# A new order of all steps for attention and a feed-forward layer on one core, with the loads of a pair's values cut into three steps

## The chip, the cores and the metric

The kernel runs on one core of one Trainium2 chip. The metric is the device time of one execution in microseconds (us). Three executions of the kernel before took 1015.79, 1017.2 and 1020.79 us; the median is 1017.2 us.

The core has five engines that each take their instructions in program order and meet only at semaphores: PE (matrix products; its weight loads are listed apart as PEld), DVE (elementwise work and reductions), ACT (exponential, Gelu, copies), POOL (more elementwise work, and a few DMA issues) and SP, which here only issues DMAs.

## The reference

The reference is sliding-window attention with 32 global tokens (8 batches, 8 heads, 512 local tokens, head size 64, window 32), followed by a feed-forward layer of 4352 tokens:

```
s_g  = scale * q_g @ concat(k_g, k_l)^T          # global rows see everything
out_g = softmax(s_g) @ concat(v_g, v_l)
s_l  = concat(scale * q_l @ k_g^T, where(|i-j| <= 32, scale * q_l @ k_l^T, -1e9))
out_l = softmax(s_l) @ concat(v_g, v_l)
x = concat(out_g, out_l) with the heads side by side      # 4352 x 512
h = x @ w_in                                     # 512 -> 2048
out = (0.5 * h * (1 + erf(h / sqrt(2)))) @ w_out # 2048 -> 512
```

All data are float32 and all of it is computed.

## The kernel before

**Tiling.** The attention is cut into 64 units (batch, half of the 512 tokens, pair of heads). A unit loads keys, queries and values, transposes keys and queries, makes scores on PE (`s`, L893), masks them with a running maximum on DVE (L912), takes exponentials on ACT (`a_t`, L766), normalises on DVE, transposes the weights on PE (`t`, L967 to L970), copies and splits them on ACT and DVE (`at`, L597 and L987) and multiplies by the values (`o`, L1004). Products are done in three parts, high*high, high*low and low*high, so every operand is copied (high part) and subtracted (low part) first. The global rows have steps of their own (`gu_*`).

**The feed-forward layer** is cut into 17 blocks of 256 tokens: 16 (batch, half) blocks and one for all global tokens. The first five take the plain way (`h`, L1193 or L1197 to L1199). The other twelve go in six groups of two blocks, in which a seven-product scheme is used: 28 products per group (`ml_p`, `hb`, L1301), each of 12 matmuls, and each with a tile `rt` of prepared weights, 512 KB, read from DRAM by one DMA of SP (`r_l`, L1262) into one of four buffers. So there are 168 `rt` loads, and one can go out only when the product four earlier has ended. The second product of the layer (`acc`, L1339 in the first block, L1347 to L1349 after) goes on between them.

**The loads.** SP issues nearly all DMAs, in one queue: keys and queries of a unit (four DMAs each, L713 and L718, rows of 32 floats), values of two units (`load_v`, `vr`, nine DMAs, L738 to L749: two of 128 rows, three and four of short rows), values for the global rows (`gu_load`, six DMAs, L1118 and L1120), the weights (`wraw`, L622 and L626, 512 KB each) and `rt`.

**What sets the order.** `plan` lists all steps: engine, what a step needs, what buffers it takes and frees, a duration from `DUR`. The order itself is a table of numbers, `SEQ`, that was searched offline; the program below only reads it. Each number names a step and the engine that does it, and the steps are written out in that order, so each engine's queue is the table's order of its steps. `DUR`, `LAT`, `iss`, due times and sizes serve the search and the table of names; they change nothing in the program when the table is fixed. The eight units of the first batch go a way of their own: keys and queries are transposed on PE (`kp`, `qp`, L806 to L814) and copied out of PSUM (`kt`, `qt`, L597) in two buffers that turn round.

## Time and profile before

| what | us |
|---|---|
| median of the three runs | 1017.2 |
| lowest, highest | 1015.79, 1020.79 |
| the profiled execution's own time | 1019.66 |
| its span | 1017.0 |
| PE busy | 992.0 |
| DVE busy | 716.4 |
| ACT busy | 727.4 |
| POOL busy | 406.2 |

The span runs from the first to the last instruction; 2.66 us of the execution lie around it. The ends of matmuls are modelled, so a PE that is shown busy is not always at its pace; a wait that the profile does show on PE is lost time. TensorE's granted clock was 0.999 of full speed over the span, which is its level of 2.4 GHz.

### The profile page before, as it was taken

The numbers are of one execution on the slowest core, as the hardware profiler recorded it, in microseconds if no ns is written. First come the engines' busy times: TensorE is split into PE (matmuls) and PEld (weight loads), VectorE is DVE, ScalarE is ACT, GpSimd is POOL, SyncE is SP. The second block draws the span as 40 slices with busy tenths as digits, with TensorE's granted clock in tenths as the row PEclk, the third lists the DMA queues.
The fourth block names the chain that finished last, engine by engine and source line by source line (L and its number), as shares of the span: only waits on it lengthen the run. The fifth ranks groups of instructions, "written<-read, shape, count | busy, mean of one in ns | idle before, by whom it ended". The sixth has DMA issues, their size and how long they took to land.

```text
span 1017.0 us, 21214 instructions
## 1 busy us (share of the span) xinstructions
PE 992.0 (98%) x6712; PEld 864.1 (85%) x6712; DVE 716.4 (70%) x2220; ACT 727.4 (72%) x1709; POOL 406.2 (40%) x431
## 2 busy tenths in 40 slices
PE   6999999999999999989999999999999999999998
PEld 3877688999889987988899988898898988998986
DVE  4899887688878888768888886687978786211111
ACT  4899889777987778776788877786888776343321
POOL 6231345433355324434543455234452454225223
PEclk9999999999999999999999999999999999999999
DMA  9996133455355798875678656986378746672641
GB/s 199 293 276 165 28 70 57 106 113 123 89 143 129 205 288 244 232 212 135 164 210 234 177 136 175 255 207 176 86 215 246 205 107 190 228 258 87 217 170 36
DMA packets 307728, 175.05 MB, mean 172 GB/s; under 512 B 256256, under 2 KB 279040, under 8 KB 307616
## 3 DMA queue, kind: packets, MB, share of 16 engines
q1 hardware_dynamic: 304064, 171.07, 61.7%
q0 software_dynamic: 1344, 1.97, 0.8%
q8 instruction: 53, 0.87, 0.4%
q10 hardware_dynamic: 2208, 0.66, 0.3%
q14 instruction: 59, 0.48, 0.2%
HBM read 149.49 MB, written 24.12 MB: 171 GB/s over the span
## 4 chain that ended last, share of the span: by engine, by line
PE 76%; DMA 12%; DVE 4%; ACT 4%; SPq 3%; issue 1%; POOL 0%; DVEq 0%; ACTq 0%; POOLq 0%
PE hb L1301 17%; PE acc L1347 10%; PE acc L1348 9%; PE acc L1349 9%; PE s L893 4%; PE o L1004 4%; DMA rt<-wd 3%; PE h L1197 3%; PE h L1198 3%; PE h L1199 3%; PE t L967 2%; PE acc L1339 2%; DMA raws<-in_q_l_dram 2%; PE h L1193 2%; PE sg L1050 2%; PE go L1137 1%
## 5 line engine op out<-in xcount | busy, mean ns | idle before, releaser
L1347 PE MATMUL acc<-wh,gh 128*128 128x512 f32 x512 | 207.2, 405 | 0.1
L1349 PE MATMUL acc<-wl,gh 128*128 128x512 f32 x512 | 202.4, 395 | 0.0
L1348 PE MATMUL acc<-wh,gl 128*128 128x512 f32 x512 | 201.8, 394 | 0.2 <-POOL gl L604 0.2
L604 POOL TENSOR_TENSOR gl<-gf,gh 128x512 fp32r<-128x512 f32 x80 | 103.9, 1298 | 222.8 <-DVE gh L599 73.5
L1301 PE MATMUL hb<-fh,rt 128*128 128x256 f32 x960 | 184.8, 281 | 4.2 <-DMA rt<-wd 3.7
L1301 PEld LDWEIGHTS hb<-fh,rt 128*128 128x128 f32 x960 | 152.8, 188 | 8.5 <-ACT sgr L766 1.8
L1301 PE MATMUL hb<-fl,rt 128*128 128x256 f32 x480 | 133.4, 278 | 0.0
L766 ACT ACTIVATE a_t<-a_t,sm 128x192 f32<-128x192 f32 (+1 forms) x256 | 116.8, 458 | 2.7 <-DVE sm L918 2.0
L1349 PEld LDWEIGHTS acc<-wl,gh 128*128 128x128 f32 x512 | 96.1, 188 | 21.7
L1347 PEld LDWEIGHTS acc<-wh,gh 128*128 128x128 f32 x512 | 96.4, 188 | 16.0 <-ACT ob L597 0.9
L1348 PEld LDWEIGHTS acc<-wh,gl 128*128 128x128 f32 x512 | 96.5, 188 | 14.4 <-POOL gl L604 0.8
L604 POOL TENSOR_TENSOR vs<-vr,vs 128x512 fp32r<-128x512 f32 x56 | 72.3, 1290 | 81.2 <-ACT vs L597 16.6
L912 DVE CUSTOM_DVE_ANT_0 a_t<-s,mask 128x192 f32<-128x192 f32 (+1 forms) x256 | 81.1, 368 | 19.1 <-PE s L893 18.5
L1301 PEld LDWEIGHTS hb<-fl,rt 128*128 128x128 f32 x480 | 90.3, 188 | 1.4
L766 ACT ACT_TABLE_LOAD x69 | 88.5, 1283 | 1.2
L987 DVE TENSOR_TENSOR at<-t,at 128x512 fp32r<-128x512 f32 (+1 forms) x112 | 68.3, 618 | 21.3 <-ACT at L597 20.2
L604 POOL TENSOR_TENSOR gl<-gq,gh 128x512 fp32r<-128x512 f32 x47 | 61.2, 1302 | 50.4 <-ACT gh L597 19.1
L597 ACT ACTIVATE at<-t 128x512 fp32r<-128x512 f32 (+1 forms) x112 | 59.8, 541 | 25.4 <-PE t L968 12.0
L1301 PE MATMUL hb<-xf,rt 128*128 128x256 f32 x576 | 75.0, 281 | 1.7 <-ACT s L597 1.6
L1301 PEld LDWEIGHTS hb<-xf,rt 128*128 128x128 f32 x576 | 70.8, 188 | 5.1 <-ACT s L597 2.0
L1197 PE MATMUL h<-xh,wh 128*128 128x256 f32 x256 | 74.9, 292 | 0.0
L1004 PE MATMUL o<-at,vs 128*128 128x256 f32 x448 | 71.8, 284 | 0.9 <-DVE gsm L1083 0.6
(191 smaller groups left out, 2287.7 us busy)
## 6 DMA issues: line engine op xcount, KB each, us to landing
rt<-wd SPq DMA_DIRECT2D x168, 512.0 KB, 4.5
wraw<-in_moe_w_in_dram SPq DMA_DIRECT2D x16, 512.0 KB, 6.9
wraw<-in_moe_w_out_dram SPq DMA_DIRECT2D x16, 512.0 KB, 6.0
raws<-in_v_l_dram SPq DMA_DIRECT2D x64, 128.0 KB, 3.2
out_dram<-ob SPq DMA_DIRECT2D x32, 256.0 KB, 2.5
raws<-in_k_l_dram SPq DMA_DIRECT2D x224, 36.0 KB, 2.6
raws<-in_q_l_dram SPq DMA_DIRECT2D x224, 32.0 KB, 2.5
vr<-in_v_l_dram SPq DMA_DIRECT2D x48, 128.0 KB, 3.7
```

The lines of the kernel that those rows point to most:

```text
L597: nc.scalar.activation(out=out, in_=in_, func=AF.Copy)
L604: (nc.vector if e == "v" else nc.gpsimd).tensor_sub(**kw)
L766: nc.scalar.activation(func=func, **kw)
L893: nc.tensor.matmul(out=st[u, "s", jj][:, c:c + w], lhsT=qq[pr, qt * P:qt * P + P], rhs=kk[pr, k0:k0 + w], start=(i == 0 and n == 0), stop= ...
L912: nc.vector.tensor_tensor_reduce(out=a_t[:, j, aoff[half][i]:aoff[half][i] + w], in0=s[:, c:c + w], in1=masks[half][i], scale=1.0, scalar= ...
L987: nc.vector.tensor_sub(out=at[:, 1], in0=st.pop((u, "t", j))[:, :n * P].rearrange("p (n q) -> p n q", q=P), in1=at.bitcast(F32)[:, 0])
L1004: nc.tensor.matmul(out=o[:, :, qsl], lhsT=l.rearrange("p s e -> p (s e)"), rhs=r, start=(n == 0), stop=(n == 3), skip_group_check=True)
L1197: nc.tensor.matmul(out=h, lhsT=hi, rhs=xh, start=(c == 0 and f % 2 == 0), stop=False, skip_group_check=True)
L1301: nc.tensor.matmul(out=h[:, r], lhsT=a, rhs=b, start=(i in (1, 5) and r == 0 and c == 0 and n == 0), stop=(c == 1 and n == 2), skip_group_ ...
L1347: nc.tensor.matmul(out=acc[t], lhsT=gh[:, f % 2, tsl], rhs=hi, start=(f == 0), stop=False)
L1348: nc.tensor.matmul(out=acc[t], lhsT=gl[:, f % 2, tsl], rhs=hi, start=False, stop=False)
L1349: nc.tensor.matmul(out=acc[t], lhsT=gh[:, f % 2, tsl], rhs=lo, start=False, stop=(f == NF - 1))
```

## The change

`DUR` and the two latencies of the search get other values (most durations of ACT and DVE 0.07 to 0.08 us lower, the latency behind a PE step 0.16 instead of 0.4), issues of late loads are counted a little longer, and the whole of `SEQ` is another table. The values of a pair of units, nine DMAs in one step, become three steps of two, three and four DMAs, which the table can put apart; the values of the global rows, six DMAs, become two steps of two and four. No instruction of PE is added or removed; a few steps change their engine.

```diff
 DUR = {
-    "k2": 0.49,
+    "k2": 0.42,
 ...
-LAT = {"t": 0.4}
-LAT0 = 0.15
+LAT = {"t": 0.16}
+LAT0 = 0.13
 ...
 SEQ = (
 ...
-    "eLcG}`+sUo5k3"
 ...
-        return (0.47 if c >= 16 else 0.55) * n
+        if name[0] in ("lv", "glv"):
+            return 0.55 * n
+        return (0.5 if c >= 16 else 0.55) * n
 ...
-            step(("lv", u), "load_v", (u, 2), "s", f0 - 18.0, [("o", units[n - 2], 1)], [("vr0", u), ("vr1", units[n + 1])], issues=9, size=0.5, after=("lv", pu if n == NPV else units[n - 2]))
-            step(("vm", u), "st_vm", (u, 2), "p", f0 - 8.0, [("lv", u)])
+            step(("lv", u, 0), "load_v", (u, 2, 0), "s", f0 - 18.0, [("o", units[n - 2], 1)], [("vr0", u), ("vr1", units[n + 1])], issues=2, size=0.3, after=("lv", pu) if n == NPV else ("lv", units[n - 2], 2))
+            for j in (1, 2):
+                step(("lv", u, j), "load_v", (u, 2, j), "s", f0 - 18.0 + j, [("lv", u, 0)], issues=2 + j, size=0.08, after=("lv", u, j - 1))
+            step(("vm", u), "st_vm", (u, 2), "p", f0 - 8.0, [("lv", u, j) for j in range(3)])
 ...
-    def load_v(e, u, n=1):
+    def load_v(e, u, n=1, part=None):
 ...
-        for t in range(2):
+        for t in range(2) if part in (None, 0) else ():
 ...
-        for r0, src, s0, m in ef:
+        for r0, src, s0, m in ef if part in (None, 1) else ():
 ...
-        for r0, src, s0 in ed:
+        for r0, src, s0 in ed if part in (None, 2) else ():
 ...
-    def gu_load(e, g, i):
+    def gu_load(e, g, i, part):
 ...
-        for j in range(2):
+        for j in range(0 if part else 2):
 ...
-        for n in range(4):
+        for n in range(4 if part else 0):
```

Three places show what the new table does. In the rows below a line of the program's body has a number six higher now than before.

The first place is ACT's queue at the program's start: `qt` and `kt` are the copies of transposed queries and keys out of PSUM, `gs` is the high part of the global queries. Before:

```order
L799 DMA raws<-in_q_l_dram 128x4x64 x2
L799 DMA rawb<-in_q_l_dram 128x4x64 x2
L597 ACT_TABLE_LOAD
L597 ACTIVATE kt<-kp 128x320
L861 ACTIVATE gs<-qg 64x4x32 x2
L597 ACTIVATE qt<-qp 128x256
L597 ACTIVATE kt<-kp 128x320
```

And now:

```order
L805 DMA raws<-in_q_l_dram 128x4x64 x2
L603 ACT_TABLE_LOAD
L603 ACTIVATE qt<-qp 128x256
L805 DMA rawb<-in_q_l_dram 128x4x64 x2
L603 ACTIVATE qt<-qp 128x256
L603 ACTIVATE kt<-kp 128x320
L867 ACTIVATE gs<-qg 64x4x32 x2
L603 ACTIVATE kt<-kp 128x320
```

Both copies of queries now stand ahead of `gs`, and the issue of the second pair's queries (`rawb`) stands behind the first of them.

The second place is SP's queue at the start: `raws` and `rawb` are the keys of the first and the second pair, `wraw` the raw weights. Before:

```order
L792 DMA raws<-in_k_l_dram 64x2x64 x2
L728 DMA qg<-in_q_g_dram 32x4x32 x4
L622 DMA wraw<-in_moe_w_in_dram 128x4x256 x3
L789 DMA rawb<-in_k_l_dram 128x4x64
L789 DMA rawb<-in_k_g_dram 32x4x64
L789 DMA rawb<-in_k_l_dram 96x4x64
L792 DMA rawb<-in_k_l_dram 64x2x64 x2
L799 DMA raws<-in_q_l_dram 128x4x64 x2
```

And now:

```order
L798 DMA raws<-in_k_l_dram 64x2x64 x2
L628 DMA wraw<-in_moe_w_in_dram 128x4x256
L734 DMA qg<-in_q_g_dram 32x4x32 x4
L795 DMA rawb<-in_k_l_dram 128x4x64
L795 DMA rawb<-in_k_g_dram 32x4x64
L795 DMA rawb<-in_k_l_dram 96x4x64
L798 DMA rawb<-in_k_l_dram 64x2x64 x2
L628 DMA wraw<-in_moe_w_in_dram 128x4x256
L805 DMA raws<-in_q_l_dram 128x4x64 x2
```

Two of the three weight tiles that stood ahead of the second pair's keys are behind them, and one stands ahead of the global queries.

The third place is SP's queue at the end of the first group of products and the start of the second (the product for which PE waits at 437 us in the profile before takes the first of the two `rt` in the row with x2). Before:

```order
L1262 DMA rt<-wd_131 128x1024
L713 DMA raws<-in_k_l_dram 32x9x32 x4
L1262 DMA rt<-wd_132 128x1024
L718 DMA raws<-in_q_l_dram 32x8x32 x4
L1262 DMA rt<-wd_132 128x1024 x2
L738 DMA vr<-in_v_l_dram 128x4x64 x2
L746 DMA vr<-in_v_l_dram 32x4x64
L746 DMA vr<-in_v_g_dram 32x4x64
L746 DMA vr<-in_v_l_dram 64x4x64
L749 DMA vr<-in_v_g_dram 32x2x64 x2
L749 DMA vr<-in_v_l_dram 32x2x64 x2
L1262 DMA rt<-wd_132 128x1024
```

And now, from the `rt` that is the second row with `rt` above:

```order
L1268 DMA rt<-wd_132 128x1024
L724 DMA raws<-in_q_l_dram 32x8x32 x4
L1268 DMA rt<-wd_132 128x1024
L719 DMA raws<-in_k_l_dram 32x9x32 x4
L744 DMA vr<-in_v_l_dram 128x4x64 x2
L1268 DMA rt<-wd_132 128x1024
L1175 DMA xg<-gc 128x32
L1268 DMA rt<-wd_132 128x1024
L752 DMA vr<-in_v_l_dram 32x4x64
L752 DMA vr<-in_v_g_dram 32x4x64
L752 DMA vr<-in_v_l_dram 64x4x64
L1268 DMA rt<-wd_132 128x1024
```

The nine issues of values no longer stand in one run between two `rt`: `rt` loads go between its parts, and the four key loads have moved behind the `rt` that PE waited for.

## Rows read from the trace of the kernel before

**Rows 1.** The page, part 1: busy time, share of the span, instructions.
```profile
PE 992.0 (98%) x6712; PEld 864.1 (85%) x6712; DVE 716.4 (70%) x2220; ACT 727.4 (72%) x1709; POOL 406.2 (40%) x431
```

**Rows 2.** Windows: length, busy of PE, PEld, DVE, ACT, POOL, clock, DMA share, GB/s.
```profile
0.00:25.00 25.00, 16.38 (x55) 9.69 (x55) 10.17 (x40) 10.91 (x30) 15.80 (x38) 1.00 0.91 198
25.00:75.00 50.00, 50.00 (x303) 38.12 (x301) 44.75 (x149) 45.44 (x119) 16.23 (x27) 1.00 1.03 285
75.00:125.00 50.00, 49.43 (x262) 34.87 (x261) 45.05 (x127) 44.80 (x93) 11.73 (x14) 1.00 0.43 104
...
350.00:475.00 125.00, 118.56 (x853) 105.61 (x850) 100.07 (x310) 94.18 (x221) 43.06 (x42) 1.00 0.81 229
475.00:850.00 375.00, 371.72 (x2622) 330.24 (x2621) 302.27 (x962) 297.94 (x715) 164.91 (x164) 1.00 0.69 184
850.00:1000.00 150.00, 149.30 (x957) 132.81 (x956) 32.39 (x65) 50.50 (x97) 48.41 (x39) 1.00 0.56 184
```

**Rows 3.** Waits of PE: who for whom, us in total, times, longest.
```profile
PE qp L814 <- DMA raws<-in_q_l_dram: 4.6, 2, 4.2
PE hb L1301 <- DMA rt<-wd: 3.7, 4, 1.6
PE hb L1301 <- ACT s L597: 1.6, 1, 1.6
...
PE kp L806 <- DMA rawb<-in_k_l_dram: 1.2, 1, 1.2
```

**Rows 4.** Timeline of 7 to 20 us: start, length, instruction, idle before it.
```profile
6.81 1.54 SPq L622 DMA_DIRECT2D wraw<-in_moe_w_in_dram  x3
...
10.47 0.64 ACT L861 ACTIVATE gs<-qg 64x128 fp32r<-64x128 f32 x2 [2.58 <-DVE qg L852]
...
10.91 1.94 SPq L792 DMA_DIRECT2D rawb<-in_k_l_dram  x2
...
11.13 0.38 ACT L597 ACTIVATE qt<-qp 128x256 f32<-128x256 f32 x1
...
11.57 0.69 PE L806 MATMUL kp<-ident,raws 128*128 128x128 f32 x2 [1.25 <-ACT qt L597]
...
19.06 0.45 PE L806 MATMUL kp<-ident,rawb 128*128 128x128 f32 x1 [1.19 <-DMA rawb<-in_k_l_dram]
```

**Rows 5.** Timeline of 430 to 448 us, SP's issues and PE's two waits.
```profile
430.01 0.87 SPq L1262 DMA_DIRECT2D rt<-wd  x2
...
430.97 2.18 SPq L738 DMA_DIRECT2D vr<-in_v_l_dram  x2
...
435.30 2.22 SPq L749 DMA_DIRECT2D vr<-in_v_g_dram  x2
...
437.32 0.36 PE L1301 MATMUL hb<-fh,rt 128*128 128x256 f32 x1 [1.64 <-DMA rt<-wd]
...
440.12 0.37 SPq L1262 DMA_DIRECT2D rt<-wd  x1
...
447.29 0.36 PE L1301 MATMUL hb<-fh,rt 128*128 128x256 f32 x1 [1.37 <-DMA rt<-wd]
```

**Rows 6.** The page, parts 2 and 6: packets; issues, KB, us to landing.
```profile
DMA packets 307728, 175.05 MB, mean 172 GB/s; under 512 B 256256, under 2 KB 279040, under 8 KB 307616
...
rt<-wd SPq DMA_DIRECT2D x168, 512.0 KB, 4.5
```

**Rows 7.** Groups by line, ACT's table loads: count, busy, mean ns, idle before.
```profile
L766 ACT ACT_TABLE_LOAD x69 | 88.5, 1283 | 1.2
```

**Rows 8.** Waits of DVE for key loads: us in total, times, longest.
```profile
DVE kt L775 <- DMA raws<-in_k_l_dram: 12.9, 6, 3.7
```

**Rows 9.** Timeline of 430 to 445 us: one hand-off from PE over ACT to DVE.
```profile
430.48 0.27 PE L968 MATMUL t<-ident,ge 128*128 128x128 f32 x1
...
430.95 0.60 ACT L597 ACTIVATE at<-t 128x512 fp32r<-128x512 f32 x1
...
431.59 0.69 DVE L987 TENSOR_TENSOR at<-t,at 128x512 fp32r<-128x512 f32 x1 [0.31 <-ACT at L597]
```

More of the change, by code (lines that the diff above doesn't have):

```diff
@@ L28 @@
 DUR = {
-    "tk": 0.62,
+    "tk": 0.55,
     "tkn": 0.75,
     "tqn": 0.45,
-    "tq": 0.44,
-    "tg": 0.32,
-    "k1": {"a": 0.47, "v": 0.33},
-    "k2": 0.49,
-    "q1": {"v": 0.3, "a": 0.41},
-    "q2": 0.42,
-    "tgh": 0.62,
-    "tgl": 0.62,
+    "tq": 0.37,
+    "tg": 0.25,
+    "k1": {"a": 0.39, "v": 0.26},
+    "k2": 0.42,
+    "q1": {"v": 0.23, "a": 0.33},
+    "q2": 0.35,
+    "tgh": 0.54,
+    "tgl": 0.55,
     "s": 0.859,
-    "m": 0.66,
-    "b": 0.17,
+    "m": 0.59,
+    "b": 0.1,
     "sg": 0.25,
-    "sgc": 0.4,
-    "sga": 0.44,
-    "e": 0.91,
-    "n": 1.11,
-    "nf": {"p": 1.2, "v": 0.42},
-    "ns": {"p": 0.8, "v": 0.28},
+    "sgc": 0.32,
+    "sga": 0.37,
+    "e": 0.83,
+    "n": 1.04,
+    "nf": {"p": 1.2, "v": 0.35},
+    "ns": {"p": 0.8, "v": 0.21},
     "t0": 0.354,
     "t1": 0.245,
-    "ah0": 0.6,
-    "al0": 0.68,
-    "ah1": 0.48,
-    "al1": 0.55,
+    "ah0": 0.52,
+    "al0": 0.61,
+    "ah1": 0.4,
+    "al1": 0.48,
     "vm": 0.45,
-    "vc": {"v": 0.42, "a": 0.63},
-    "vl": {"p": 1.3, "v": 0.65},
+    "vc": {"v": 0.35, "a": 0.55},
+    "vl": {"p": 1.3, "v": 0.58},
     "o": 0.466,
@@ L62 @@
     "sg0": 0.55,
-    "ao0": {"a": 0.54, "v": 0.61},
-    "ao1": {"a": 0.4, "v": 0.48},
+    "ao0": {"a": 0.46, "v": 0.54},
+    "ao1": {"a": 0.32, "v": 0.41},
     "o0": 1.8,
-    "c0": {"a": 0.8, "v": 0.85},
-    "c": 0.4,
-    "x": 0.87,
-    "gmin": 0.9,
-    "gex": 0.75,
-    "gn": 0.88,
-    "gt": 0.464,
-    "gah": 0.38,
-    "gal": 0.417,
-    "gagh": 0.27,
-    "gagl": 0.269,
-    "gvc": {"v": 0.45, "a": 0.73},
-    "gvl": {"p": 1.57, "v": 0.85},
+    "c0": {"a": 0.72, "v": 0.78},
+    "c": 0.32,
+    "x": 0.8,
+    "gmin": 0.83,
+    "gex": 0.67,
+    "gn": 0.81,
+    "gt": 0.464,
+    "gah": 0.3,
+    "gal": 0.347,
+    "gagh": 0.19,
+    "gagl": 0.199,
+    "gvc": {"v": 0.38, "a": 0.65},
+    "gvl": {"p": 1.57, "v": 0.78},
     "go": 0.584,
-    "gsh": 0.277,
-    "gsl": 0.282,
+    "gsh": 0.197,
+    "gsl": 0.212,
     "gx": 0.027,
-    "gyh": 0.42,
-    "gyl": 0.4,
-    "xh": {"v": 0.36, "a": 0.42},
-    "xl": {"v": 0.43, "p": 0.75},
+    "gyh": 0.34,
+    "gyl": 0.33,
+    "xh": {"v": 0.29, "a": 0.34},
+    "xl": {"v": 0.36, "p": 0.75},
     "h": 1.4,
     "hc": 0.352,
-    "g": 0.6,
-    "gh": {"a": 0.62, "v": 0.43},
-    "gl": {"p": 1.3, "v": 0.68},
+    "g": 0.52,
+    "gh": {"a": 0.54, "v": 0.36},
+    "gl": {"p": 1.3, "v": 0.61},
     "mo": 1.382,
-    "ob": 0.597,
-    "w1": {"a": 0.59, "v": 0.36},
+    "ob": 0.517,
+    "w1": {"a": 0.51, "v": 0.29},
     "hc0": 0.435,
@@ L217 @@
+    "!L`IXBpqubr5(BsYlo|&v!kyg&@tSR=-@}^baZu;N2x9NsH{cZvLRC0vbtk)$NY}}b!>?&=@{u4>sZ^drK6!G)Y2TCi0qEUTP7oiB5f_twK$?(E%RC~v|MZHZCTKAtL1LXqn1T2`B8LqNz2lfWi7O5"
+    "ag-AsYgyG&87+-gN7uD%Y}wkfqs1F-ipHav=$@ASEr(m4iJoZbiT)?LAo~9$kXcU"
 )
```

181 lines of the change are left out of this document (91 added, 90 removed).

## The prediction

> **What bounds the kernel now.** I read the page's first part, then the windows, then PE's waits, and the timeline last. PE is busy 992.0 of 1017.0 us [rows 1], so it is the engine to watch, and what a new order can win is first of all the 25 us that it stands idle. The windows say where these lie [rows 2] (the first number of a row is the window's length, the second PE's busy time). In 0 to 25 us PE lacks 25.00 - 16.38 = 8.62 us. In 25 to 75 it lacks nothing, in 75 to 125 it lacks 0.57. In 350 to 475 it lacks 125.00 - 118.56 = 6.44, the worst stretch of the middle; in 475 to 850, three times as long, 3.28; in 850 to 1000 only 0.70. These make 19.6 of the 25 us; the rest is 125 to 350 and the last 17 us, which I take as unmoved. The stretch of 350 to 475 is also where DMAs work hardest after the start, 0.81 of their time at 229 GB/s.
>
> PE's waits name the causes [rows 3]: 4.6 us for the first queries (one of 4.2, the very first landing, which no order moves), 3.7 us in four waits for `rt`, 1.6 us in one wait for an ACT copy, 1.2 for the second pair's keys. The timeline shows how the `rt` waits come about [rows 5]. SP issues two `rt` at 430.01, then a run of value loads: the two of 128 rows hold its queue for 2.18 us, two short ones later for 2.22, and the next `rt` goes out at 440.12. PE waits 1.64 us at 437.32 for one of the two `rt` issued at 430.01, more than 7 us before, although such a load lands after 4.5 us in the median [rows 6]; it waits 1.37 us again at 447.29. So an order that sends `rt` earlier, and does not put nine other issues between two of them, has something to win, but a small thing: all moveable waits that the profile shows are 19.6 - 4.2 = 15.4 us, 1.5% of the span.
>
> A busy PE may hide more. The full pace is that of 850 to 1000 us, where PE idles 0.70 us and PEld is busy 132.81 of 150.00, a share of 0.885. In 350 to 475 the share is 105.61/125.00 = 0.845; at 0.885 it would need 119.3 us, which leaves 5.7 us, no more than the idle time of 6.44. The Trainium skill ("Perfetto Trace Analysis", section Identifying the Most-Contended Engine) says that matmul busy time is a bad measure of the distance to the limit and that the share of weight loads is the better one. Read against 100%, that share would promise 19 us in this stretch alone; the trace disagrees, since even the stretch without waits ends at 0.885, and the sum keeps to the 6 us.
>
> **The change part by part.** No matmul is added or removed, so PE's work stays, and only waits can come and go.
>
> The start. Before, ACT makes `gs` (10.47, 0.64 us) ahead of the copy `qt` at 11.13, and `gs` itself waits for the global queries; PE's next transpose waits for that copy until 11.57, 1.25 us [rows 4]. In the new order both `qt` stand ahead of `gs`, so the 1.25 us go. The second pair's keys stood behind three weight tiles of 512 KB (issued from 6.81) and their last part was issued from 10.91; PE waits for them, 1.19 us before 19.06 [rows 4]. Now two of these tiles stand behind: at the 285 GB/s at which the DMAs run in 25 to 75 us [rows 2], 2 x 0.524 MB are 3.7 us less in front of the keys, more than the wait. Against it: one weight tile (1.8 us by the same rate) stands ahead of the global queries, and the second pair's queries are issued behind a copy on ACT instead of at once; both feed steps that have since moved back on PE. What is late next is the conversion of weights on DVE and ACT, which are busy 0.90 and 0.91 of 25 to 75 us [rows 2]: time won at 20 us is partly waited away before 125. Of 2.4 us I keep 2.0, counting the two shorter waits for copies beside them; the ends are 0 (all waited away) and -4.4 (all of 8.62 but the first 4.2).
>
> The middle, 350 to 475. In the new order the four key issues that stood before the two `rt` are behind the first of them, and the nine value issues are split, with `rt` between. Four issues at the 0.43 us of each of the two `rt` (0.87 for two [rows 5]) are 1.7 us, so this `rt` leaves about 1.7 us earlier, as much as the 1.64 that PE waited; the `rt` after the values leave earlier by the whole run, more than 1.37. Over the whole queue, runs of nine or more issues between two `rt` fall from 34 to 20. The 1.6 us behind an ACT copy falls in this stretch too; the product that waits stands farther behind it now. Of 6.44 I take -4.0; ends 0 and -6.
>
> The rest, 475 to 1000: 3.28 + 0.70 idle, of which 0.7 are `rt` waits (3.7 less the two above). I take -1.0; ends +3 (a new order makes new small waits) and -3.
>
> What it costs. The new order has 74 table loads on ACT where there were 70: 4 x 1.283 = 5.1 us [rows 7], on an engine idle for 28% of the span. DVE gets 34 more instructions and POOL 11 fewer. These lie beside PE's work; they cost when a hand-off comes late. One hand-off of PE's transposes to the next matmul takes from 430.48 to 432.28, 1.80 us [rows 9]. PE's matmuls between the two ends of a hand-off, counted at their pace, are about as many as before; two of 112 hand-offs now have only some 1.4 us of them, where the least was 1.8. That is 2 x 0.4; I take +0.5, ends 0 and +8 (the rival below).
>
> Late keys and queries show on DVE (12.9 us of waits for keys [rows 8]) and not on PE; they become shorter and are worth nothing by themselves.
>
> The sum: -2.0 - 4.0 - 1.0 + 0.5 = -6.5 us. Against the profiled execution, 1019.66 us (span 1017.0 and 2.66 around it), that is 1013.2. The median of the runs is 2.46 lower, so I predict 1017.2 - 6.5 = 1010.7 us.
>
> **The rivals.**
>
> *The transfers bind, not their order.* If `rt` is late because the DMAs are full, earlier issues only wait longer in flight. For it: the load issued at 430.01 took over 7 us, and 256,256 of 307,728 packets are under 512 B [rows 6], none of which the change removes. Against it: 0.81 and 229 GB/s in this stretch, where 25 to 75 us shows 1.03 and 285 [rows 2]. Then the middle and rest give nothing and the start half: 1017.2 - 1.0 + 0.5, about 1016.5. The Trainium skill speaks for this rival ("DMA: Bandwidth & Descriptors", sections Why small descriptors are slow (HBM only) and Issuing engines are not separate DMA queues): small descriptors pay a fixed overhead each, and all issuers share the same 16 DMA engines. By that rule the `rt` waits would stay at 3.7 us; the trace bears it out for the flight of single loads, and not for the stretch.
>
> *ACT holds PE up, and it is slower.* The place is the attention's stretch from 125 to 850 us. A table load that stands right before a copy that PE needs delays it by 1.28 us, and a hand-off has 1.80 us to hide [rows 7, 9]; the one wait of 1.6 us for an ACT copy [rows 3] shows that it happens. If seven of the 74 stand so, with no spare matmuls between, that is 7 x 1.28 = 9 us, and more than the 6.5 us won once it is above five. At seven, with the start alone won, the time is 1017.2 - 1.0 + 9, some 1025. Against it: 69 table loads were there before and PE waited so once.
>
> *More comes free than the idle time.* From 25 to 125 us the conversions on DVE and ACT (0.90 busy) set the pace while PE is shown busy throughout, at 565 matmuls in 100 us where 475 to 850 shows 7 per us [rows 2]. If the earlier start carries through, and PE there runs 10 us shorter, the time is near 1001. Little speaks for it, since the weights' transfers fill that stretch.
>
> **How the numbers follow.** A difference of 0.5%, 5.1 us, is about what a measurement of this kernel can tell from none; the forecast stands only a little beyond it. I give the forecast's case 0.57, with its own range of 1006 to 1016 (of it 0.41 are faster than 1012.1, 0.16 within), the bound transfers 0.15 (all within), the slower case 0.23 (0.20 slower, 0.03 within), the larger gain 0.05 (faster). That makes faster 0.46, same 0.34, slower 0.20. The range of 8 in 10 is 1003 to 1024: it leaves out most of the larger gain and the worse half of the slower case.
>
> **What would show it.** Right: in the profile after, PE's waits for `rt` below 1 us in all; PE's idle time in the first 25 us near 6 us, with no wait for `qt` copies or `rawb` keys over 0.5; PE's idle time in 350 to 475 near 2 us; issues of values in parts with `rt` between. Wrong in the middle: `rt` issued earlier and landing no earlier. Wrong in what it costs: new waits of PE for ACT or DVE, `at`, `gl` or `s`, of 5 us and more in total, with a table load ahead of them. Wrong at the start: the 25 us won, and PE's idle time back between 50 and 125 us in waits for `wf`.

## The result and the profile after

The changed kernel takes 1022.87 us (median of five executions, 1020.36 to 1024.92) against 1017.2 for the kernel before: a ratio of 1.0051, with a 95% interval of 1.0028 to 1.0073. A second measurement, beside 29 executions of the kernel before, gave 1022.94 us and 1.0042 (1.0025 to 1.0059). So it is slower by about 0.45%, some 5 us, where 6.5 us less were forecast. The time lies inside the stated range of 1003 to 1024, but only because that range is wide: the forecast's sign was wrong.

The profiled execution took 1022.87 us with a span of 1020.8. The page's first part, in answer to [rows 1]:

```profile
PE 993.9 (97%) x6712; PEld 861.8 (84%) x6712; DVE 734.3 (72%) x2254; ACT 722.4 (71%) x1690; POOL 395.6 (39%) x420
```

The windows of [rows 2] (length, busy time of PE, PEld, DVE, ACT and POOL, clock, DMA share, GB/s), with 125 to 350 us beside them:

```profile
0.00:25.00 25.00, 14.25 (x48) 8.78 (x49) 7.56 (x34) 8.00 (x22) 10.24 (x28) 1.00 0.80 193
25.00:75.00 50.00, 48.61 (x294) 35.92 (x293) 41.62 (x139) 44.97 (x120) 17.61 (x32) 1.00 0.97 281
...
125.00:350.00 225.00, 221.98 (x1584) 198.10 (x1583) 191.93 (x588) 177.21 (x417) 94.53 (x96) 1.00 0.44 106
350.00:475.00 125.00, 123.86 (x902) 111.38 (x902) 104.71 (x312) 97.08 (x227) 47.48 (x46) 1.00 0.87 240
475.00:850.00 375.00, 370.09 (x2600) 326.72 (x2599) 312.25 (x997) 292.09 (x703) 155.57 (x152) 1.00 0.70 183
```

The kernel before in the window that the forecast took as unmoved:

```profile
125.00:350.00 225.00, 224.45 (x1625) 203.25 (x1625) 179.74 (x566) 182.07 (x437) 101.97 (x106) 1.00 0.46 111
```

PE's idle time (length less PE's busy time) rose in the first 25 us from 8.62 to 10.75 us, in 25 to 75 from nothing to 1.39, in 125 to 350 from 0.55 to 3.02, and in 475 to 850 from 3.28 to 4.91. In 350 to 475 it fell from 6.44 to 1.14, as forecast. PE's waits, in answer to [rows 3] (us in total, times, longest):

```profile
PE qp L820 <- DMA raws<-in_q_l_dram: 4.5, 2, 4.2
PE kp L812 <- ACT qt L603: 4.2, 1, 4.2
PE qp L820 <- DMA rawb<-in_q_l_dram: 2.0, 1, 2.0
PE o L1010 <- DVE at L993: 1.5, 4, 0.5
PE sg L1056 <- DVE sm L918: 1.2, 1, 1.2
PE go L1143 <- DVE sm L918: 1.1, 1, 1.1
...
PE sg L1056 <- DVE gc L1171: 0.7, 1, 0.7
PE hb L1307 <- ACT hb L603: 0.7, 2, 0.4
```

The waits for `rt` and for the keys `rawb` are gone. New are one of 4.2 us for the copy `qt`, one of 2.0 for the second pair's queries, and several for DVE. The first two, in the timeline of 4 to 16 us (start, length, instruction, idle time before it), in answer to [rows 4]:

```profile
4.32 1.94 SPq L734 DMA_DIRECT2D qg<-in_q_g_dram  x4
...
5.45 0.39 ACT L603 ACTIVATE qt<-qp 128x256 f32<-128x256 f32 x1 [2.28 <-PE qp L820]
...
8.44 2.14 ACTq L805 DMA_DIRECT2D rawb<-in_q_l_dram  x2
...
10.20 0.37 ACTq L805 DMA_DIRECT2D rawb<-in_q_l_dram  x1
...
10.62 0.39 ACT L603 ACTIVATE qt<-qp 128x256 f32<-128x256 f32 x1 [4.78 <-DMA qg<-in_q_g_dram]
...
11.06 0.69 PE L812 MATMUL kp<-ident,raws 128*128 128x128 f32 x2 [4.18 <-ACT qt L603]
...
15.95 0.90 PE L820 MATMUL qp<-ident,rawb 128*128 128x128 f32 x3 [1.98 <-DMA rawb<-in_q_l_dram]
```

After its first copy ACT comes to the issue of the second pair's queries. In the program each of these two DMAs waits for the semaphore of an earlier DMA (the DMAs of SP and ACT share eight). The first goes out at 8.44, when one load of the global queries `qg` has landed (8.41), the second at 10.20, when the last of them has (10.18). The row at 10.20, from a narrower window, is the second of the two in the row at 8.44: the issues themselves take 0.38 and 0.37 us, and the rest of the 2.14 is waiting. ACT works in order, so the second copy of queries, whose input is ready before 6 us, runs at 10.62, and PE waits for it; then PE waits again for the queries issued so late.

The other new loss, in the timeline of 328 to 344 us. `sw` and `ss` are sums of weights that DVE makes for the prepared tiles, `wd<-sl` is the store of such a tile:

```profile
328.93 0.38 SPq L1264 DMA_DIRECT2D wd<-sl  x1
...
329.01 0.86 DVE L1235 TENSOR_TENSOR sw<-wh,wl 128x512 f32<-128x512 f32 x1
...
332.19 0.69 DVE L1235 TENSOR_TENSOR sw<-wh,wl 128x512 f32<-128x512 f32 x1 [2.32 <-DMA wd<-sl]
...
334.39 0.35 DVE L918 CUSTOM_DVE_ANT_0 a_t<-s,mask 128x192 f32<-128x192 f32 x1
...
335.21 0.71 PE L1143 MATMUL go<-vgs,agt 128*128 128x256 f32 x4 [1.11 <-DVE sm L918]
...
340.56 0.69 DVE L1235 TENSOR_TENSOR sw<-wh,wl 128x512 f32<-128x512 f32 x1 [1.89 <-DMA wd<-sh]
...
343.29 0.50 PE L1056 MATMUL sg<-k,gs 128*128 128x288 f32 x2 [0.74 <-DVE gc L1171]
```

The second `sw` takes the buffer that the store frees. The store goes out at 328.93 and lands 3.2 us later; DVE stands still for 2.32 us with four more sums and the masks queued behind, and PE waits for the masks (`sm`) at 335.21. The same happens 8 us later ahead of `gc`.

The clock of the first 25 us has to be read from PE's own rows. In this trace the rows of the granted clock begin at 25.5 us, so the 1.00 of the first window, and the 0.999 over the span told ahead of the prediction, say nothing of the time before. The same two products, before and after that point:

```profile
22.31 1.33 PE L1056 MATMUL sg<-kt,gs 128*128 128x288 f32 x2
...
29.59 0.65 PE L1056 MATMUL sg<-kt,gs 128*128 128x288 f32 x2
```

They take twice as long at first, which is the pace of the lower of the two levels, 1.2 GHz. The clock rows begin at 25.5 us in the first profile of either kernel, and between 21 and 32 us in the other runs. Up to there PE is busy 14.8 us in the changed kernel and 16.9 in the kernel before, so the half pace costs some 7.4 and 8.4 us (an estimate from these numbers). It is a large part of the loss at the start in both, and not what sets them apart.

**A finer measure.** The rows of two kernels are hard to compare when one runs behind the other. So I give each matmul the time from its start to the next start that its shape and line have when nothing waits (0.229 us for 128x512, 0.109 to 0.114 for 128x128 and 128x256, 0.075 and 0.090 for the scores; 0.429 and 0.216 in the first block, L1345 and L1199). The sum over the kernel is 939 us, the same for both. "PE's loss" in a stretch of this work is the real time that it took, less the work. Worked out from the starts of all matmuls, in us:

| order of the steps | 0-20 | 20-102 | 102-160 | 160-280 | 280-320 | 320-411 | 411-749 | 749-939 |
|---|---|---|---|---|---|---|---|---|
| before, first profile | 19.2 | 5.8 | 2.3 | 5.6 | 1.6 | 10.7 | 18.9 | 4.4 |
| before, second (e12) | 17.1 | 9.3 | 2.3 | 4.8 | 1.6 | 8.4 | 20.8 | 4.6 |
| changed, first | 21.4 | 6.5 | 4.1 | 5.3 | 5.2 | 5.0 | 19.0 | 6.0 |
| changed, second (e8) | 22.1 | 6.5 | 4.1 | 5.3 | 5.2 | 6.7 | 18.0 | 6.1 |
| e2, queries on SP | 17.2 | 6.5 | 4.1 | 5.7 | 5.1 | 5.8 | 19.1 | 6.1 |
| e6, old to 320 | 17.6 | 6.4 | 2.3 | 4.8 | 1.6 | 8.3 | 16.0 | 6.1 |
| e9, old 280 to 320 | 21.6 | 6.4 | 4.1 | 5.2 | 1.7 | 7.4 | 16.9 | 6.3 |
| e11, values joined | 21.9 | 6.5 | 4.2 | 5.3 | 8.4 | 7.5 | 39.9 | 6.3 |
| e13, three undone | 17.4 | 11.9 | 2.3 | 5.2 | 1.6 | 7.3 | 17.1 | 6.2 |
| e15, old, queries late | 26.1 | 5.2 | 2.3 | 4.8 | 1.6 | 8.8 | 20.9 | 4.9 |

Two things stand in it. Some stretches repeat to 0.1 us whenever the order is the same (102 to 160, 280 to 320); others differ by 2 to 4 us between two executions of one order (the start, 320 to 749). And the new order against the old, as means of two profiles: +3.6, -1.1, +1.8, 0, +3.6, -3.7, -1.4, +1.5, together about +4.5 us. The middle's win is there; three losses ahead of it are larger. The columns on both sides of 411 are best read together, since a wait of 1 to 2 us falls now before that point and now behind it: 29.6, 29.2 and 29.7 us where the order is old from 320 to 749 (before, e12, e15), 24.0 to 24.9 where it is new (both of the changed kernel, e2, e6, e9, e13), and 47.4 in e11.

### The profile page after: what moved, and what is told of

It reads as the page before. It is cut to its first block, busy times and chain, and to the rows that moved or that the text cites. A ratio compares the mean times of both kernels' runs of the same rounds, so it can differ in the third digit from the quotient of the medians.

```text
span 1020.8 us, 21196 instructions
## 1 busy us (share of the span) xinstructions
PE 993.9 (97%) x6712; PEld 861.8 (84%) x6712; DVE 734.3 (72%) x2254; ACT 722.4 (71%) x1690; POOL 395.6 (39%) x420
## 4 chain that ended last, share of the span: by engine, by line
PE 76%; DMA 6%; ACT 6%; DVE 6%; SPq 3%; issue 2%; POOL 0%; DVEq 0%; ACTq 0%; POOLq 0%
PE hb L1307 19%; PE acc L1353 10%; PE acc L1354 10%; PE acc L1355 9%; PE s L899 4%; PE o L1010 4%; PE t L973 3%; DMA rt<-wd 2%; PE h L1203 2%; PE h L1199 2%; PE h L1204 2%; PE h L1205 2%; PE sg L1056 2%; PE acc L1345 2%; PE go L1143 2%
## 5 line engine op out<-in xcount | busy, mean ns | idle before, releaser
L1355 PEld LDWEIGHTS acc<-wl,gh 128*128 128x128 f32 x512 | 96.2, 188 | 21.7
L610 POOL TENSOR_TENSOR gl<-gq,gh 128x512 fp32r<-128x512 f32 x47 | 62.1, 1322 | 59.0 <-DVE gh L605 17.2
L603 ACT ACTIVATE at<-t 128x512 fp32r<-128x512 f32 (+1 forms) x112 | 60.3, 541 | 26.2 <-PE t L976 11.8
```

The lines of the kernel that those rows point to most:

```text
L603: nc.scalar.activation(out=out, in_=in_, func=AF.Copy)
L610: (nc.vector if e == "v" else nc.gpsimd).tensor_sub(**kw)
L1355: nc.tensor.matmul(out=acc[t], lhsT=gh[:, f % 2, tsl], rhs=lo, start=False, stop=(f == NF - 1))
```

## The experiments

The orders of before and of the change have been done by nearly the same steps at many points (three to five of 4511 differ). So a kernel can take one order up to such a point and the other from there (the point is called a seam); all run with the changed kernel's functions. "New" is the changed kernel's order, "old" that of before, and points are given in us of PE's work. Ratios are against executions of the kernel before on the same chip, with 95% intervals.

**e1: the second pair's queries issued first (new order).** ACT's queue:

```diff
 L805 DMA raws<-in_q_l_dram 128x4x64 x2
+L805 DMA rawb<-in_q_l_dram 128x4x64 x2
 L603 ACTIVATE qt<-qp 128x256
-L805 DMA rawb<-in_q_l_dram 128x4x64 x2
 L603 ACTIVATE qt<-qp 128x256
```

> The changed kernel with one step put back: ACT issues the second pair's queries (two DMAs, L805) at once, ahead of its first copy, as the kernel before does; every other step stays. Theory A (the start lost time because these two DMAs stand in ACT's in-order queue behind a copy, there wait for earlier DMAs to land, and hold up the second copy of queries): PE's waits of 4.2 us for the `qt` copy and of 2.0 us for the queries themselves both fall below 0.5 us; PE's idle time in the first 25 us falls from 10.75 to 5 to 8 us; the time falls by 2 to 4 us, from 1022.9 to about 1020. Rival B (the start is only shifted: the conversion of the weights sets the pace from 25 to 125 us, and what is won at 10 us is waited for later): the two waits go, but the idle time comes back before 125 us and the time stays within 1 us of 1022.9. Rival C (the loss lies elsewhere, in hand-offs between DVE, ACT and PE after 125 us, and the profiled start is an accident of one execution): the time stays at 1022.9.

Measured: 1020.94 us, ratio 1.0031 (1.0014 to 1.0049), 2 us below the changed kernel but with intervals that overlap. Both waits went and the idle time of the first 25 us is 8.4 us, but a new wait came (profile of e1, 12 to 14 us):

```profile
12.56 0.64 ACT L867 ACTIVATE gs<-qg 64x128 fp32r<-64x128 f32 x2 [5.17 <-DVE gs L677]
...
13.23 0.44 ACT L603 ACTIVATE kt<-kp 128x320 f32<-128x320 f32 x1
...
13.72 0.69 PE L820 MATMUL qp<-ident,rawb 128*128 128x128 f32 x2 [3.77 <-ACT kt L603]
```

ACT now stands at `gs`, which waits for the global queries, and the second copy of keys, for which PE waits 3.77 us, is queued behind. The DMA was one item in the wrong place of ACT's queue; the next took its part.

**e2: the same queries issued by SP, at the same place (new order).** ACT has no DMA between its copies:

```diff
 L734 DMA qg<-in_q_g_dram 32x4x32 x4
+L805 DMA rawb<-in_q_l_dram 128x4x64 x2
 L795 DMA rawb<-in_k_l_dram 128x4x64
```

> The changed kernel, in which SP and not ACT issues the second pair's queries, at the same place of the order: behind the global queries, ahead of the second pair's keys. So ACT has no DMA between its two copies of queries, while the data still come late, and the second pair's keys leave SP about 1 us later. Theory A in its first half (ACT is blocked by an issue that waits): PE's wait of 4.2 us for the `qt` copy falls below 0.5 us; the queries land at 9 to 11 us instead of 15.9, so their wait of 2.0 us goes too; the time falls by 1.5 to 4 us from 1022.9, like the run in which they are issued first. If only lateness of the data counts and not the blocking: the wait for the `qt` copy stays at 3 us or more. Rivals B and C: no change of the time, 1022.9 within 1 us.

Measured: 1019.93 us, ratio 1.0019 (1.0003 to 1.0035), 3 us below the changed kernel. These intervals overlap as well; but set directly against the twelve executions of e8 on the same chip, the mean is 3.2 us lower (2.0 to 4.5), and that of e1 2.0 lower (1.0 to 3.1). Profile of e2:

```profile
5.45 0.81 ACT L603 ACTIVATE qt<-qp 128x256 f32<-128x256 f32 x2 [2.27 <-PE qp L820]
...
6.28 0.98 SPq L805 DMA_DIRECT2D rawb<-in_q_l_dram  x2
...
10.88 0.45 PE L820 MATMUL qp<-ident,rawb 128*128 128x128 f32 x1 [1.60 <-DMA rawb<-in_q_l_dram]
```

Both copies run at once, the queries leave at 6.28 and are there at 10.88, 5 us earlier, and the loss of the first 20 us falls from 21.7 to 17.2. So it was the waiting issue on ACT that cost; the wait for the queries themselves, expected to go too, stays (2.2 us in two waits). The Trainium skill ("DMA: Bandwidth & Descriptors", section Issuing engines are not separate DMA queues) says that issuing on several engines saves only the time to initiate, which is usually small beside the DMA. The trace agrees on the issue itself, 0.38 and 0.37 us on ACT. What cost here was not that time but the waits of the two issues, 2.6 and 1.4 us, for ACT stood still meanwhile with a copy behind them that PE waited 4.18 us for.

**e3: old start (old to 102, then new).** `order = old[:545] + rest of new`.

> The order of the kernel before up to the step at which PE has done its first 102 us of work, and from there the new order (the steps done by then differ by four in the two orders). Theory A (the whole start of the new order costs 2.5 to 3.6 us at that point, where the two profiles lie so far apart): the time is 1022.9 - 3 = about 1020, and the idle time in 0 to 25 us is that of before, 8.6 us. Rival B (what is lost at the start is hidden later): 1022.9 within 1 us. If more than the one DMA is wrong with the new start, this run is faster than the one with the queries issued first by 1 us or more.

Measured: 1019.51 us, ratio 1.0019 (1.0003 to 1.0035), as much as e2. It is 1.4 us below e1, more than the 1 us set as the sign of a second fault; but e1 has a wait of its own, for `kt`, and against e2, which has no such wait, nothing beside the queries shows as wrong with the new start.

**e4: new middle only (old, new from 355 to 412, old).** `order = old[:1855] + new[:2164] + old`, each step where it comes first.

> The order of the kernel before, with the new order only from 355 to 412 us of PE's work (about 398 to 460 us of the execution), where the values' loads are split and `rt` goes between them. Theory D (the middle of the forecast was right: the waits for `rt` and their surroundings cost 5 to 6.5 us before, and the rest of the new order takes them back): the time is 1017.2 - 5.5 = about 1012, PE's idle time in 350 to 475 us falls from 6.4 to 1 to 2 us, and PE's waits for `rt` fall from 3.7 us to about 0.7. Rival E (time won in the middle is given back later by itself, since what follows waits for ACT and DVE): the idle time in 350 to 475 us falls, the idle time after 475 us rises by as much, and the time stays at 1017.2 within 1.5 us.

Measured: 1020.53 us, ratio 1.0025 (1.0007 to 1.0042): slower than before. The win did not come at all; the loss in 320 to 411 is 11.8 us in its profile, of it 6.9 in 320 to 355, ahead of the seam. The idle time in 350 to 475 us did not fall either (118.67 of 125 us busy), so both theories missed: the stretch did not do behind the old order what it does behind the new one. Why the run is slower than the kernel before stays open.

**e5: the sums behind the masks (new order).** DVE's queue near 330 us; the same near 340 with `gc`:

```diff
 L1235 TENSOR_TENSOR sw<-wh,wl 128x512
-L1235 TENSOR_TENSOR sw<-wh,wl 128x512
-L1235 TENSOR_TENSOR ss<-sw 128x256
...
 L918 ISA a_t_133,sm<-s,mask_110 128x192
...
 L924 TENSOR_SCALAR sm<-sm 128x4
+L1235 TENSOR_TENSOR sw<-wh,wl 128x512
+L1235 TENSOR_TENSOR ss<-sw 128x256
...
```

> The changed kernel with one stretch of DVE's queue put in another order, near 330 and 340 us: two groups of sums for the prepared weights (`sw` and `ss`, L1235 and L610), which stand ahead of the masks of one unit and of the copy `gc` of the global rows, go behind them; nothing else moves but the copies and stores that depend on these sums. In the profile of the changed kernel DVE stands still twice ahead of a `sw`, 2.3 us at 332.19 and 1.9 us at 340.56, until a store of prepared weights (`wd`) has landed and so given its buffer back, and then PE waits for the masks (`sm`, 1.1 us) and for `gc` (0.7 us). Theory F (these two waits of DVE are what costs PE its 3.5 us between 318 and 360 us): PE's waits `go` for `sm` and `sg` for `gc` fall below 0.3 us, PE's loss over its pace between 280 and 320 us of its work falls from 5.2 to 2 us, the time falls by 2 to 3.5 us from that of the changed kernel. Rival G (what is lost there is made good by 412 us of work, since the values' and `rt` loads, sent earlier, hold PE up in the middle if it arrives sooner): the waits go, but between 320 and 412 us of work PE loses as much more, and the time stays within 1 us.

Measured: 1025.86 us, ratio 1.0068 (1.0042 to 1.0093): slower still. The wait for `sm` ahead of `go` went, but the second group made a longer one (profile of e5):

```profile
342.67 0.39 DVE L1171 TENSOR_TENSOR gc<-gx,gc 64x32 f32<-64x32 f32 x2 [3.33 <-ACT gc L1165]
...
350.07 0.71 PE L1010 MATMUL o<-at,vs 128*128 128x256 f32 x4 [3.56 <-DVE at L993]
```

DVE now stood 3.33 us at `gc` with the sums behind it, and the copy `at` came late; two waits for `rt`, 2.1 us, came back besides. It shows what an item of DVE's queue that waits does to PE; it does not show that the store was the cause.

**e6 and e7: old to 320, then new to the end; old to 320, new to 412, then old.** `old[:1686] + rest of new`, and `old[:1686] + new[:2164] + old`.

> The order of the kernel before up to 320 us of PE's work (near 359 us of the execution) and the new order from there, where the two orders differ by five steps. If the parts add up (theory H): the new order's losses before that point (7 to 8 us in the profiles) go and its win of the middle stays, so the time is 7 us below the changed kernel's, 1014 to 1016, below the kernel before by 2 to 4 us. Rival G (the win of the middle is only the making good of what was lost before it, since it is PE's late arrival that gave the loads their time): the middle wins 1 to 3 us instead of 6, and the time is that of the kernel before or more, 1018 to 1020.

> The order of the kernel before, with the new order from 320 to 412 us of PE's work (about 359 to 460 us of the execution): the middle stretch of the new order from 35 us earlier than in the run that took it from 355. Theory H (the parts add up, and the run from 355 lost its win at the seam): 5 to 6 us faster than the kernel before, about 1012. Rival G (the middle's win depends on what came before): within 2 us of the kernel before, PE's loss over its pace between 320 and 412 us of its work 8 to 11 us as in the kernel before, not the 5 to 6 of the changed one.

Measured: e6 1014.04 us, ratio 0.9966 (0.9946 to 0.9986), 8.9 us below the changed kernel; e7 1016.27 us, 0.9985 (0.9966 to 1.0004), no difference that can be told. What the new order loses lies before 320, and e6 is what adding up the parts gave (1014 to 1016). In 320 to 411 the loss is 8.3 and 9.2 us against 5.0 and 6.7 behind the new start, which looks as if the middle won less. Taken in steps of 15 us (worked out anew from the same starts, with 0.113 us for 128x256), the difference stands right behind the seam: from 320 to 335 it is 1.9 us in e6 and 2.7 in e14, where the changed kernel has 0.1 and the old order 0.8 to 2.1. From 335 to 410 e6 and e14 lose 4.2 and 4.3 us, just as the changed kernel does (4.3 in both profiles), and the old order 9.1, 6.7 and 6.1 (before, e12, e15). So the middle's win does not hang on what was lost ahead of it, but for some 2 us at its beginning; whether these are the seam's, or what a PE that arrives later no longer waits for, was not told apart. (e7 shows 6.1 there: a wait that e6 has behind 410 us falls before it.)

**e8: the changed kernel again.** No edit.

> The changed kernel itself once more, on the chip on which these runs stand, to tell how far executions of one kernel lie apart and where. If the first measurement holds: 0.3 to 0.7% slower than the kernel before, 1020 to 1024. If one execution's profile tells the kernel's time: PE's loss over its pace in each stretch of its work is that of the first profile within 0.3 us. If the stretches differ by a us and more between two executions of the same kernel, these are the ones that hang on transfers, and a stretch's gain is only to be believed from several profiles.

Measured: 1022.94 us, as told above. Its waits of 4.4 us for `qt` and of 1.2 us for `sm` stand again; the loss in 320 to 411 is 1.7 us more, that in 411 to 749 1.0 less.

**e9: old only from 280 to 320.** `new[:1464] + old[:1686] + new`.

> The changed kernel with the order of the kernel before only from 280 to 320 us of PE's work (about 318 to 365 us of the execution), where the new order loses 5.2 us over PE's pace and the old one 1.6. Theory H (the parts add up): 5.2 - 1.6 = 3.6 us below the changed kernel, about 1019. Theory G' (a part of such a loss is made good in the next stretch, because what arrives later waits less for transfers, DVE and ACT): the loss in 280 to 320 is 1.6 us, but that of 320 to 411 rises from 5 to 6.5 us towards the 8.3 that it had behind the old order; then the time is 1 to 2 us below the changed kernel, about 1021.5.

Measured: 1019.65 us, ratio 1.0025 (1.0010 to 1.0039), 3.3 us below the changed kernel, though on another chip; by the ratios it is 1.7 us. So the time does not tell whether all of the 3.6 us is kept. The loss there is 1.7 instead of 5.2 us; that of 320 to 411 rose to 7.4, but with 411 to 749 it is 24.3, as in the changed kernel.

**e10: old to 320, new to 749, old.** `old[:1686] + new[:3941] + old`.

> The order of the kernel before up to 320 us of PE's work, the new order from there to 749 us (about 819 us of the execution), and the old one again to the end. Against the run that keeps the new order to the end: in 749 to 939 us of work the new order loses 2.4 + 3.55 = 6.0 us over PE's pace, the old one 1.36 + 2.98 = 4.3. If the parts add up: 1014.0 - 1.6, about 1012.4, and 0.5% below the kernel before. If the seam costs what the run from 355 lost at its seam: 1014 to 1015.

Measured: 1015.78 us, ratio 0.9983 (0.9967 to 0.9998): not better than e6. The last stretch won its 1.5 us; 411 to 749 shows 23.7 us of loss against 16.0 in e6. The order there is that of e6, so the seam at 749 is not the cause: the profile is of the slowest of e10's twelve executions (1019.28 us), in which PE waits 3.3 us for POOL's `vs` at 549 us and then runs 3.4 us at a granted clock of 0.50.

**e11: the values joined again (new order).** In SP's queue the parts follow one another as before; the other engines' queues stay as they are:

```diff
 L744 DMA vr<-in_v_l_dram 128x4x64 x2
+L752 DMA vr<-in_v_l_dram 32x4x64
+L752 DMA vr<-in_v_g_dram 32x4x64
+L752 DMA vr<-in_v_l_dram 64x4x64
+L755 DMA vr<-in_v_g_dram 32x2x64 x2
+L755 DMA vr<-in_v_l_dram 32x2x64 x2
 L1268 DMA rt<-wd_132 128x1024
 L1175 DMA xg<-gc 128x32
 L1268 DMA rt<-wd_132 128x1024
-L752 DMA vr<-in_v_l_dram 32x4x64
-L752 DMA vr<-in_v_g_dram 32x4x64
-L752 DMA vr<-in_v_l_dram 64x4x64
 L1268 DMA rt<-wd_132 128x1024
-L755 DMA vr<-in_v_g_dram 32x2x64 x2
-L755 DMA vr<-in_v_l_dram 32x2x64 x2
```

> The changed kernel with the values' loads joined again: the second and third part of each pair's values (and the second part of the global rows' values) issued right behind the first, as the kernel before does; runs of nine and more issues between two `rt` on SP rise from 19 to 27. Theory of the forecast (a run of nine issues between two `rt` makes PE wait for `rt`): PE's waits for `rt` rise from 0.2 us to 2 to 4 us, PE's loss in 372 to 411 us of work from 2.1 to 4 or 5 us, and the time to about 1026. Rival (the splitting does nothing by itself; `rt` comes in time in the new order because it stands earlier): within 1 us of the changed kernel, 1023, with waits for `rt` below 1 us.

Measured: 1048.68 us, ratio 1.0299 (1.0276 to 1.0321). Far more than either theory gave. The profile of e11, near 330 and 480 us, and two of PE's waits:

```profile
329.44 1.91 SPq L1126 DMA_DIRECT2D raws<-in_v_g_dram  x4
...
333.23 0.38 SPq L1264 DMA_DIRECT2D wd<-sl  x1
...
336.00 0.69 DVE L1235 TENSOR_TENSOR sw<-wh,wl 128x512 f32<-128x512 f32 x1 [5.03 <-DMA wd<-sl]
...
339.02 1.20 PE L1143 MATMUL go<-vgs,agt 128*128 128x256 f32 x4 [4.06 <-DVE sm L918]
...
485.11 0.54 DVE L781 STREAM_TRANSPOSE kt<-raws 128x160 f32<-128x160 f32 x2 [4.31 <-DMA raws<-in_k_l_dram]
```

```profile
PE hb L1307 <- DMA rt<-wd: 8.3, 8, 1.7
...
PE sg L1056 <- DVE sm L918: 3.9, 1, 3.9
```

and the window behind the longer wait (the clock is the third number from the end):

```profile
337.60:344.40 6.80, 5.38 (x19) 4.73 (x20) 5.06 (x17) 5.79 (x13) 3.05 (x2) 0.50 0.54 152
```

It gives the larger dose that e5 failed to take away. The four loads of global values now stand ahead of the store, which leaves at 333.23 instead of 328.93; DVE's wait at `sw` grows from 2.32 to 5.03 us and PE's wait at `go` from 1.11 to 4.06. At 485 us it is keys that come late, DVE stands 4.31 us, and PE waits 3.9 for the masks. `rt` costs 8.3 us in eight waits. Each of the two long waits for the masks also took the clock down: it was 0.50 for 6.8 us from 337.6 and for 3.4 us from 487.8. PE was working for 5.4 and 3.4 us of that, at half pace, so some 4.4 us of the 26 are the clock's (an estimate). In this order the splitting matters. The old order has the joined values and no wait as long, the first landing aside: 1.7 us for `sm` is the longest in e12, and `rt` has 3.7 us in its first profile and none in e12. Why it bears the joined values was not tried; other steps stand elsewhere in it.

**e12: the old order in the changed kernel's functions.** `order = old`, each pair's three parts in a row.

> The table of the kernel before in the changed kernel's functions: the same order, with the values' loads as three steps that follow one another at once. It changes no instruction. The time is that of the kernel before within its interval, 1018. Its profile is a second one of the old order, to see which of its losses stand in every execution: if 320 to 411 us of PE's work shows 10 to 11 us of loss again, the waits for `rt` belong to the old order; if it shows 8 to 9, as the two runs with the new order in this stretch behind the old one did, 2 us of the middle's win were an accident of the one profile from which the forecast was made.

Measured: 1018.1 us, ratio 0.9998 (0.9981 to 1.0015). Its window of 350 to 475 us and two of PE's waits from the head of the list:

```profile
350.00:475.00 125.00, 120.78 (x870) 107.99 (x869) 101.76 (x314) 96.92 (x230) 45.27 (x46) 1.00 0.82 233
```

```profile
PE sg L1056 <- DVE sm L918: 3.4, 3, 1.7
PE hb L1307 <- ACT s L603: 1.8, 2, 1.6
```

No wait for `rt` stands in its list at all, where the first profile of the same order had four with 3.7 us [rows 3]; the idle time of the window is 4.2 us instead of 6.44. Instead it waits 3.4 us for `sm`. So the `rt` waits, 3.0 of the 4.6 us on which the forecast's middle rested, belong to that one execution. The third, 1.6 us for an ACT copy, stands in both profiles and is gone in the changed kernel.

**e13: three places undone.** New, with the queries on SP, old from 102 to 160 and from 280 to 320: `new'[:545] + old[:834] + new'[:1464] + old[:1686] + new'`.

> The new order with three of its places undone at once, each alone already tried or read: the second pair's queries issued by SP instead of ACT (that run was 3 us below the changed kernel), the old order from 102 to 160 us of PE's work (loss over PE's pace there 4.1 us in the new order, 2.3 in the old), and the old order from 280 to 320 (that run was 3.3 us below the changed kernel). If these three places are the whole of what the new order loses: 1022.9 - 3 - 1.8 - 3.3 = 1014.8, as much as the run with the old order up to 320 us (1014.0), and 0.2 to 0.5% below the kernel before. If a part of each loss is made good later by the waits that it saves: 1016 to 1018, no better than the kernel before.

Measured: 1019.13 us, ratio 1.0007 (0.9992 to 1.0022): clearly below the changed kernel and level with the kernel before, 4 us short of the sum. At the first seam it has a wait of its own (profile of e13):

```profile
124.43 1.42 DVE L610 TENSOR_TENSOR wl<-wf,wh 128x512 fp32r<-128x512 f32 x2 [2.52 <-POOL wl L610]
...
127.21 0.92 PE L1101 MATMUL gt<-ident,sgr 128*128 128x128 f32 x4 [2.52 <-DVE sm L918]
```

```profile
127.50:130.80 3.30, 3.30 (x18) 3.30 (x17) 2.89 (x12) 1.44 (x6) 2.02 (x4) 0.50 0.08 14
```

The loss in 20 to 102 is 11.9 us, 5.4 more than in the changed kernel. The wait is 2.5 us, and behind it the granted clock is 0.50 for 3.4 us with PE busy throughout, 1.7 us more: together 4.2 us, as much as the run is short of the sum. So the three places come near the whole loss by this estimate; no run shows them without the seam.

**e14: e6 again.** No edit.

> The fastest version so far once more, against other runs of the kernel before, with a second profile: the old order up to 320 us of PE's work, the new one behind it. If its gain is real: 0.1 to 0.5% faster than the kernel before, about 1014.5, with no wait of PE for the masks `sm` ahead of the global rows' products before 360 us and a loss of 8 to 9 us over PE's pace in 320 to 411 us of work. If it was chance: within 0.1% of the kernel before.

Measured: 1015.28 us, ratio 0.9979 (0.9962 to 0.9996): the gain of 0.2 to 0.3% over the kernel before stands. Its profile loses some 2 us more in 320 to 749 than that of e6.

**e15: the start's fault put into the old order.** The queries behind ACT's first copy, and behind the global queries on SP:

```diff
-L805 DMA rawb<-in_q_l_dram 128x4x64 x2
 L603 ACTIVATE kt<-kp 128x320
+L805 DMA rawb<-in_q_l_dram 128x4x64 x2
 L867 ACTIVATE gs<-qg 64x4x32 x2
```

> The start of the new order's fault built into the kernel before: its own order, with the second pair's queries issued on ACT behind the first copy of keys, and behind the global queries on SP, instead of first. Theory A (an issue on ACT that follows a copy waits there for the landing of an earlier DMA, here the global queries', and the data come late): the first of the two issues goes out only when global queries have landed, near 8 to 10 us, the queries land at 13 to 16 us, PE waits for them 3 to 6 us, and the time is 3 to 5 us above the kernel before, about 1022. If such a loss at the start is made good later: the wait is there and the time is within 1.5 us of the kernel before.

Measured: 1022.57 us, ratio 1.0057 (1.0041 to 1.0074), 4.6 us above the kernel before, as expected. The way was another (profile of e15):

```profile
5.73 1.53 SPq L628 DMA_DIRECT2D wraw<-in_moe_w_in_dram  x3
...
7.29 1.32 ACTq L805 DMA_DIRECT2D rawb<-in_q_l_dram  x2
...
16.66 0.45 PE L820 MATMUL qp<-ident,rawb 128*128 128x128 f32 x1 [9.40 <-DMA rawb<-in_q_l_dram]
```

The two issues took 1.32 us, hardly held, but the data took over 9 us; three weight tiles of 512 KB had been issued just before, where it was one in e2. PE waited 9.4 us; the loss of the first 20 us is 26.1 against 17 to 19, that of 20 to 102 is 5.2 against 5.8 and 9.3. The time rose by 4.6 us, so about half was made good.

## Why the prediction was wrong

**The start: -2.0 forecast, +2.5 measured (0 to 102).** The two gains were right: PE waits neither for the copy behind `gs` nor for the keys `rawb`. The step that failed was "Against it": the second pair's queries "are issued behind a copy on ACT instead of at once", priced at nothing because the steps that they feed had moved back on PE. I priced the data and not ACT's queue: the issue waits, and everything behind it on ACT waits with it (4.2 us), and the data were late too (2.0). e2 shows it by taking the 4.2 away, e15 that late queries cost the old order 4.6 us as well.

**The middle: -4.0 forecast, -3.7 between the means (320 to 411).** The profile after shows what was forecast, `rt` without waits and 1.14 us idle, and the new order wins some 3 us from 335 to 410 behind either start (e6, e14). But that the size came out was luck in part. The term was sized on one execution: of the 4.6 us of waits that it names, the 3.0 for `rt` do not stand in the old order's second profile, and only the 1.6 for an ACT copy does. What else the new order wins there was not traced to a cause.

The reading of how `rt` came late was wrong as well, and by the same step as at the start. I took the 2.18 and 2.22 us as the time that value loads hold SP's queue. Most single issues take 0.3 to 0.75 us, and the rest is waiting for an earlier DMA to land. In the kernel before, the `rt` issued at 430.01 lands at 437.19, and only then does the next short load go out (the last row is from SP's own waits over the whole kernel: us in total, times, longest):

```profile
430.01 7.18 DMA rt<-wd
...
437.20 0.31 SPq L749 DMA_DIRECT2D vr<-in_v_g_dram  x1
...
SPq L749 <- DMA rt<-wd: 6.4, 8, 1.3
```

**The rest: -1.0 forecast, about 0 measured** (-1.4 and +1.5). The -1.4 is within what two executions differ by; the +1.5 repeats in every row with the new order.

**The costs: +0.5 forecast, +5.4 measured** (1.8 in 102 to 160, 3.6 in 280 to 320), inside the ends of 0 and +8. This is the slower rival's place and nearly its size, but not its mechanism: beside the wait at the start, PE waits for ACT only in small pieces (0.7 us for `hb` the largest sum). In 280 to 320 it is DVE, which waits for a store to land so that a sum may take its buffer. e9 shows the place and e11 the mechanism, with a larger dose (and a fall of the clock besides); taking that wait away alone, by one more buffer, was not tried, and e5 did not manage it by order. In 102 to 160 DVE does four subtractions of weights in a row (3.37 us) ahead of a copy that PE needs; that was read from the timeline and only undone together with other things (e6, e13).

**"Late keys and queries show on DVE and not on PE ... worth nothing by themselves"**: wrong as a rule. It holds while DVE has slack; in e11 a wait of 4.31 us for keys became 3.9 us on PE.

**The transfers bind**: not in this stretch. With the DMAs busier than before (0.87 and 240 GB/s in 350 to 475 us, against 0.81 and 229) PE idled 1.14 us.

So the start and the costs, 4.5 and 4.9 us beside the forecast, are most of the 11 us between forecast and result.

## What to carry to other kernels

- When a step moves in an in-order queue, price what stands behind it, not only what it feeds: an issue or a sum that waits for another transfer's landing holds every later item of its engine.
- A wait of 1 to 2 us in one profile is no term of a sum until a second execution shows it: here some 5 us of the old order's 69 us of loss stood in other stretches in its second profile, while the losses that came from the order alone repeated to 0.1 us.
- Gains of neighbouring stretches add up only as far as the seam between them lets them: e6 and e14 came out at the sum, e13 4 us above it, with a wait and a fall of the clock at its seam. The best version found is the old order up to 320 us of PE's work and the new one behind it, 0.2 to 0.3% faster than the kernel before.
